# A bigger ring for raw weights, one transpose a step later, and weight loads in front of stores

## The chip, the core and the metric

The kernel runs on one core of a Trainium2 chip. The metric is the device time of one execution in microseconds (us). Five engines work side by side, each through its own list of instructions in order: TensorE (PE, with its weight loads as PEld), VectorE (DVE), ScalarE (ACT), GpSimd (POOL) and SyncE (SP), which here issues nearly all DMA transfers. They wait for each other by semaphores.

## The reference

Attention with a forget-gate bias, then a gated feed-forward layer, then a plain one, on 2304 tokens of width 512:

```python
def _attn_ref(q, k, v, s):                       # q, k, v: (4, 8, 576, 64)
    scores = scale * np.matmul(q, k.transpose(0, 1, 3, 2))
    cum = np.cumsum(np.maximum(s, 0.0), axis=-1)
    bias = -(cum[:, :, :, None] - cum[:, :, None, :])
    scores = np.where(causal, -1000000000.0, scores + np.minimum(bias, 0.0))
    ...                                          # softmax over the last axis
    return np.matmul(attn, v)
def _moe_ref(x, w_gate, w_val, w_out):           # 512 -> 1536 -> 512
    g = x @ w_gate
    silu = g * (1.0 / (1.0 + np.exp(-g)))
    return silu * (x @ w_val) @ w_out
def _moe2_ref(x, w_in, w_out):                   # 512 -> 2048 -> 512
    h = x @ w_in
    return (h * (1.0 / (1.0 + np.exp(-h)))) @ w_out
```

## The kernel before, in words

**Three parts.** The first layer (attention and the gated layer) goes batch by batch, four batches of 576 tokens. The attention of a batch is eight *units*, two for each pair of heads: half A (query tiles 0 to 2) and half B (tiles 3 and 4). The attention of batch 0 runs alone at the start. That of each later batch runs inside the gated layer of the batch before. The second layer comes last.

**Chunks.** The gated layer's weights come in nine chunks for each batch, named c = 0 to 35 over the four batches: six gate-and-value chunks of four steps (`gate`, 24 matmuls of 288 columns a step) and three output chunks of eight steps (`down`, 12 matmuls a step). Each chunk has 96 such matmuls. Every product is made of three matmuls in a 32-bit format, of a high part and a low part of each operand.

**Weights.** They arrive as raw 64-bit words. In the first batch each chunk is loaded as four raw pieces of 512 KB (`w_load`, line 388, or `w_piece`, line 403; tile name `r`, tag `wraw`), decoded one chunk ahead (`decode`: ScalarE at lines 409 and 410, VectorE at lines 412 and 415), cut into high and low parts (`w_cut`: ScalarE at line 112, POOL at line 501, tile `wt`) and stored (`w_store`, line 489). The later batches load them back finished (`w_half`, line 396). From chunk 9 on the second layer's weights are prepared in the same manner in *sets* (`ahead_load`, `ahead`, `u_sum`, `u_cut`), and `u_store` (line 486) writes a set out in four stores.

**Rings.** A pool with n buffers hands out its tiles in turn, and a tile's first writer waits until the last reader of the tile n places earlier is done. Raw pieces, decoded tiles, sums and cut tiles all come from the one ring `raw`. The 32-bit scratch `dk` of the decode comes from the PSUM ring `ps_m` (four banks, shared with the gate and output groups `pgv` and `po`) for chunks 1 to 8, and from the pool `dec` for chunk 0 and for the sets. A gate step takes two banks of `ps_m`. ScalarE's tanh (line 531) and VectorE (lines 532 and 533) empty them. Scores (`psc`, line 218) and transposes (`ptr`, lines 302 to 316) each take the two buffers of the PSUM ring `ps_a`. ScalarE (line 112) and VectorE (line 114) copy the transposes out as `pt`.

**What sets the order.** In the loop over the chunks of the first three batches TensorE's order is that of the code: `at[k]` lists what is put in front of quarter k of chunk c. For the k-th chunk of a batch that is the scores of unit k in front of quarter 0, the values of unit k-2 and the transposes of unit k-1 in front of quarter 2. The order of the other engines is made by a scheduler, which a change in a ring moves too. In the last batch all orders are those of the code: after each step the list `todo` of that step is issued, and then the stores of sets that are ready (`stores`).

Of the kernel before, what the change touches and what calls it, by code (L numbers as in the profile page):

```python
# [66 lines left out]
def kernel(  # L67
# [11 lines left out]
    first_layer = ctx.enter_context(ExitStack())  # L79
    attention = ctx.enter_context(ExitStack())  # L80
    second_layer = ctx.enter_context(ExitStack())

    def pool(name, bufs, space=None, scope=ctx, side="left"):
        kw = {"space": space} if space is not None else {}
        return scope.enter_context(tc.tile_pool(name=name, bufs=bufs, side=side, reuse_waits="tile", **kw))
# [2 lines left out]
    const = pool("const", 1)  # L88
    dram = pool("dram", 1, bass.MemoryType.DRAM)
    wt_p = pool("wt", 4)  # L90
    raw_p = pool("raw", 5, scope=first_layer)
    dec_p = pool("dec", 2, scope=first_layer)
    tmp_p = pool("tmp", 3, scope=first_layer)
    h_p = pool("h", 6, scope=first_layer)
    xt_p = pool("xt", 8, scope=first_layer)
# [1 line left out]
    qkr_p = pool("qkr", 3, scope=attention, side="right")  # L97
    cum_p = pool("cum", 3, scope=attention, side="right")
    e_p = pool("e", 6, scope=attention, side="right")
    z_p = pool("z", 4, scope=attention, side="right")  # L100
    pt_p = pool("pt", 3, scope=attention, side="right")
    zero_p = pool("zero", 1, scope=attention, side="right")
    v_p = pool("v", 2, scope=attention, side="right")
    sm_p = pool("sm", 10, scope=attention, side="right")
    ps_m = pool("ps_m", 4, PS)
    ps_a = pool("ps_a", 2, PS, scope=attention, side="right")

# [181 lines left out]
    def turn_mm(b, g, half):  # L289
        tiles, base, n = HALF[half]  # L290
        es = st.pop((b, g, half, "e"))
        ps = [ps_a.tile([P, 2, 512], F32, tag="a", name="ptr") for _ in range(2)]
        put = []
        for j, tile, o in PLACE[half]:
            k0 = TILES[j][0]
            for i in tiles:
                q0, r = TILES[i]
                if q0 < k0:
                    continue
                for hd in range(2):  # L300
                    x = o + q0 - max(k0, base)
                    nc.tensor.transpose(ps[tile][:, hd, x : x + r], es[i][:r, hd, k0 : k0 + P], ident[:r, :r])  # L302
            off = max(k0, base) - base
            put.append((j, tile, o, off, n - off))
        for i, tile, hd, o in PLACE0[half]:
            q0, r = TILES[i]
            if b == 0:
                for k in range(2):
                    nc.tensor.matmul(
                        out=ps[tile][k * D : k * D + D, hd, o : o + r], lhsT=es[i][:r, k, :D], rhs=ident[:r, :r],  # L310
                        start=True, stop=True,
                    )
                continue
            z = st.pop((b, g, half, "z", i))
            r = P
            nc.tensor.transpose(ps[tile][:, hd, o : o + r], z[:r], ident[:r, :r])
        st[b, g, half, "p"] = (ps, put, [None, None])

    def turned(b, g, half, k):
        n = HALF[half][2]  # L320
        ps, _, pt = st[b, g, half, "p"]
        pt[k] = pt_p.tile([P, 2, 512], F32, tag="pt", name="pt")
        w = WIDE[half][k]
        if w is None:
            copy("av"[k], pt[k][:, 0, :n], ps[k][:, 0, :n])
        else:
            copy("av"[k], pt[k][:, :, :w], ps[k][:, :, :w])
# [156 lines left out]
    def u_store(q, k, e):  # L484
        name, n, *parts = wst["o", q, k]
        return nc.sync.dma_start(out=wu_d[q // 2, "ZSCE".index(name), :, e, :n], in_=parts[e])
# [86 lines left out]
    def chunk_steps(c):  # L573
        kind, i = stream[c]
        if c == 0:
            return [lambda f=f, n=n: gate(c, f, f, *n) for f, n in ((1, both[0]), (0, both[1]), (1, both[1]))]
        if kind == "gv":
            return [lambda f=f, n=n: gate(c, 2 * i + f, f, *n) for f, n in order(2, both, "01"[i == NGV - 1])]
        return [lambda m=m, n=n: down(c, i, m, *n) for m, n in order(KD, both, "1")]
# [162 lines left out]
    def scores(u):  # L742
        x = units[u]
        fetch(u)
        if (*x, "e") not in st:
            masks(*x)
        score_mm(*x)
        for i in HALF[x[2]][0]:
            for f in (score_min, expo, inverse, first_keys, normal):
                f(*x, i)  # L750

    def transpose(u):
        turn_mm(*units[u])
        turned(*units[u], 0)
        turned(*units[u], 1)

    def value(u):
        value_mm(*units[u])
        x_high(*units[u])
        x_low(*units[u])  # L760
# [57 lines left out]
    def body():  # L818
# [48 lines left out]
        for q in range(12):  # L867
            x = 17 * q // 3
# [11 lines left out]
        for c in range(last):  # L880
            b = batch[c]
            cur = chunk_steps(c)
            at = {k: [] for k in range(5)}
            if b + 1 < B:
                k, u0 = c % len(L1), (b + 1) * H
                if k < H:
                    at[1 if c == 0 else 0].append(lambda x=u0 + k: scores(x))
                    if k > 1:
                        at[2].append(lambda x=u0 + k - 2: value(x))
                    if k > 0:  # L890
                        at[2].append(lambda x=u0 + k - 1: transpose(x))
                else:
                    at[1] += [lambda x=u0 + k - 2: value(x), lambda x=u0 + k - 1: transpose(x)]
                    at[3].append(lambda x=u0 + k - 1: value(x))
            for n, stp in enumerate(cur):
                if n == 0:
                    w_ahead(c)
                if n * 4 % len(cur) == 0:
                    todo = events.get(c * 4 + n * 4 // len(cur), [])
                    with tc.issue_after(w_last[0]) if todo else nullcontext():  # L900
                        with tc.issue_after(act_last[0]) if todo else nullcontext():
                            for f in todo:
                                f()
                if c == 0:
                    for p in at[n - 1] if n else []:
                        p()
                elif n * 4 % len(cur) == 0:
                    for p in at[n * 4 // len(cur)]:
                        p()
                stp()  # L910
            for p in at[4]:
                p()
# [6 lines left out]
        stores = []  # L919
        g = nc.gpsimd  # L920
        for c in range(last, n1):
            cur = chunk_steps(c)
            k = c - last
            more = [[] for _ in range(4)]
            extra = []
            if c + 1 < n1:
                more[0] += [lambda e=e: w_half(c + 1, e) for e in range(2)]
            i = tail_pieces.get(c)
            if i is not None:
                more[1].append(lambda i=i: ahead(i))  # L930
                if i % 2:
                    more[1].append(lambda q=i // 2: u_sum(q))
                    for e in range(2):
                        more[2 + e].append(lambda q=i // 2, k=e: u_cut(q, k))
                        more[2 + e].append(
                            lambda q=i // 2, k=e: stores.extend(lambda e=e: u_store(q, k, e) for e in range(2))
                        )
            if c + 1 in tail_pieces:
                more[1].append(lambda i=tail_pieces[c + 1]: ahead_load(i))
            if k == 0:  # L940
                more[2].append(lambda: x2_load(0))
            sub = {1: 1, 2: 2, 4: 3, 5: 4}.get(k)
            cuts = {1: [0], 2: [1], 3: [2, 3], 4: [4], 5: [5], 6: [6]}.get(k, [])
            if sub:
                more[0].append(lambda: x2_sub(0, sub))
            for e, x in enumerate(cuts):
                src = None if x in (0, 2, 5) else {1: 1, 3: 2, 4: 3, 6: 4}[x]
                f = lambda x=x, src=src: x2_cut(0, x, None if src is None else p2["t", src], g)
                if len(cur) == 4:
                    more[2].append(f)  # L950
                else:
                    extra.append(f)
            if k == 7:
                more[3].append(lambda: u_load(1, "Z"))
            if k == 8:
                more[0].append(lambda: u_load(0, "ZS"))
            for n, stp in enumerate(cur):
                if n == 0:
                    wst.pop(c - 1, None)
                stp()  # L960
                todo = more[n] if len(cur) == 4 else more[n // 2] if n % 2 == 0 else extra[n // 4 : n // 4 + n // 2 % 2]
                late, stores[:] = list(stores), []
                for f in todo:
                    f()
                for f in late:
                    f()
# [100 lines left out]
```

## Time and profile before

| | us |
|---|---|
| median of 3 runs | 1007.95 |
| lowest, highest run | 1001.23, 1009.87 |
| profiled execution | 1002.95 |
| its span, first to last instruction | 1001.1 |
| TensorE busy in the span | 989.5 (99%) |
| ScalarE, VectorE, POOL busy | 523.0, 557.0, 592.7 |

The profile is of one execution. Times in it count from the start of the span. A row's busy time is that of its instructions laid over one another. "Idle before" is the time in which the engine had nothing running just before them, and the name behind the arrow is what ended it. In the trace DMA issue rows belong to SP's queue (SPq), and what a transfer takes to land is given apart from them.

### The profile page before, as it was taken

The page shows a single profiled execution, that of the slowest core. Times are in us where ns is not written, and L with a number is a line of the kernel's source. Part 1 is how long each engine was busy: PE and PEld are TensorE (multiplying, and loading weights), DVE is VectorE, ACT ScalarE, POOL GpSimd, SP SyncE. Part 2 cuts the span into 40 slices and gives each one's busy share as a digit, 9 for nine tenths or more (in the row PEclk, how much of TensorE's full clock was granted, in tenths as well). Part 3 has the DMA queues.
Part 4 walks back from the last instruction along what each step waited for, and adds up shares of the span by engine and source line. Part 5 has one row for each costly group of instructions (what it writes and reads, how often), then busy time and mean ns, then how long its engine had stood idle before and what let it go on. Part 6 is the DMA issues. An engine that isn't in the chain of part 4 may idle for free.

```text
span 1001.1 us, 19462 instructions
## 1 busy us (share of the span) xinstructions
PE 989.5 (99%) x6924; PEld 929.8 (93%) x6924; DVE 557.0 (56%) x1408; ACT 523.0 (52%) x1267; POOL 592.7 (59%) x748
## 2 busy tenths in 40 slices
PE   8999999999999999999999999999999999999998
PEld 6588889999998899899899999999999999999998
DVE  6868576635546545535542323366666667665555
ACT  6779888535666436655533443234544335543333
POOL 6967747515867556757542665356567458674445
PEclk9999999999999999999999999999999999999999
DMA  8798879667779799775858776797767866896662
GB/s 240 198 319 301 275 277 301 222 221 246 279 267 294 266 306 311 265 248 214 288 205 330 270 297 258 261 388 278 294 242 281 312 222 249 297 343 232 244 219 113
DMA packets 81616, 267.16 MB, mean 267 GB/s; under 512 B 9904, under 2 KB 29360, under 8 KB 66160
## 3 DMA queue, kind: packets, MB, share of 16 engines
q1 hardware_dynamic: 81328, 265.66, 75.8%
q8 instruction: 54, 0.88, 0.3%
q14 instruction: 42, 0.34, 0.1%
q10 hardware_dynamic: 192, 0.27, 0.1%
HBM read 208.15 MB, written 57.75 MB: 266 GB/s over the span
## 4 chain that ended last, share of the span: by engine, by line
PE 90%; ACT 3%; DMA 3%; DVE 2%; issue 1%; POOL 1%; SPq 0%; DVEq 0%; ACTq 0%; POOLq 0%
PE pgv L522 9%; PE pgv L524 9%; PE pgv L523 9%; PE pu L663 6%; PE pu L666 6%; PE pu L667 6%; PE po L708 6%; PE po L709 6%; PE po L710 6%; PE po L522 5%; PE po L523 5%; PE po L524 5%; PE pv L351 5%; PE psc L218 4%; PE ptr L302 3%; ACT e L255 1%
## 5 line engine op out<-in xcount | busy, mean ns | idle before, releaser
L522 PE MATMUL pgv<-xt,wt 128*128 128x288 f32 x768 | 229.5, 299 | 0.2 <-DVE wraw L415 0.2
L524 PE MATMUL pgv<-xt,wt 128*128 128x288 f32 x768 | 226.1, 294 | 0.0
L523 PE MATMUL pgv<-xt,wt 128*128 128x288 f32 x768 | 226.0, 294 | 0.0
L640 POOL TENSOR_TENSOR h<-u,h 128x384 fp32r<-128x384 f32 x72 | 74.8, 1039 | 142.1 <-ACT h L112 134.5
L522 PEld LDWEIGHTS pgv<-xt,wt 128*128 128x128 f32 x768 | 144.1, 188 | 11.5 <-DVE m L235 6.3
L523 PEld LDWEIGHTS pgv<-xt,wt 128*128 128x128 f32 x768 | 144.1, 188 | 0.0
L524 PEld LDWEIGHTS pgv<-xt,wt 128*128 128x128 f32 x768 | 144.0, 188 | 0.0
L112 ACT ACTIVATE h<-u 128x288 fp32r<-128x288 f32 (+1 forms) x168 | 79.8, 475 | 100.5 <-DVE u L533 99.2
L535 POOL TENSOR_TENSOR h<-u,h 128x288 fp32r<-128x288 f32 x96 | 79.0, 825 | 86.4 <-ACT h L112 84.2
L522 PE MATMUL po<-h,wt 128*128 128x288 f32 x384 | 114.7, 299 | 0.0
L523 PE MATMUL po<-h,wt 128*128 128x288 f32 x384 | 113.1, 294 | 0.0
L524 PE MATMUL po<-h,wt 128*128 128x288 f32 x384 | 113.0, 294 | 0.0
L708 PE MATMUL po<-h,wt 128*128 128x384 f32 x336 | 112.4, 335 | 0.0
L709 PE MATMUL po<-h,wt 128*128 128x384 f32 x336 | 112.3, 334 | 0.0
L710 PE MATMUL po<-h,wt 128*128 128x384 f32 x336 | 112.3, 334 | 0.0
L663 PE MATMUL pu<-x,wt 128*128 128x384 f32 x330 | 111.8, 339 | 0.1
L666 PE MATMUL pu<-x,wt 128*128 128x384 f32 x330 | 111.8, 339 | 0.0
L667 PE MATMUL pu<-x,wt 128*128 128x384 f32 x330 | 111.7, 339 | 0.0
L640 POOL TENSOR_TENSOR h<-t,h 128x384 fp32r<-128x384 f32 x96 | 107.0, 1136 | 5.5 <-ACT h L112 5.5
L669 ACT ACTIVATE s<-pu 128x384 f32<-128x384 f32 x48 | 23.6, 492 | 150.0 <-PE pu L667 150.0
L255 ACT ACTIVATE e<-e,m 64x64 f32<-64x64 f32 (+4 forms) x160 | 88.3, 554 | 25.7 <-DVE m L235 25.0
L719 DVE TENSOR_TENSOR acc<-po,acc 128x384 f32<-128x384 f32 x144 | 76.8, 558 | 36.3 <-PE po L710 35.6
(115 smaller groups left out, 2187.0 us busy)
## 6 DMA issues: line engine op xcount, KB each, us to landing
wt<-w_d SPq DMA_DIRECT2D x54, 1024.0 KB, 6.9
wt<-wu_d SPq DMA_DIRECT2D x48, 1024.0 KB, 9.2
wt<-wu_d SPq DMA_DIRECT2D x47, 768.0 KB, 6.8
r<-in_w_dram SPq DMA_DIRECT2D x36, 512.0 KB, 6.8
w_d<-wt SPq DMA_DIRECT2D x18, 1024.0 KB, 8.5
r<-in_w_dram SPq DMA_DIRECT2D x64, 256.0 KB, 7.1
qkr<-in_qk_dram SPq DMA_DIRECT2D x32, 288.0 KB, 9.0
cumb<-cum_d SPq DMA_DIRECT2D x15, 576.0 KB, 9.2
```

The costliest lines, as they stand in the source:

```text
L112: act_last[:] = [nc.scalar.activation(out=out, in_=in_, func=AF.Copy, scale=scale).ins]
L255: nc.scalar.activation(out=e[:r, hd, :wd], in_=e[:r, hd, :wd], func=AF.Exp, bias=m[hd][:r], scale=-1.0, accum_out=put[hd],)
L522: nc.tensor.matmul(out=ps[:, :n], lhsT=a, rhs=xh, start=(k == 0), stop=False)
L523: nc.tensor.matmul(out=ps[:, :n], lhsT=a, rhs=xl, start=False, stop=False)
L524: nc.tensor.matmul(out=ps[:, :n], lhsT=c, rhs=xh, start=False, stop=(k == last))
L640: nc.gpsimd.tensor_tensor(out=h[:, 1], in0=u, in1=h[:, 0].bitcast(F32), op=ALU.subtract)
L663: nc.tensor.matmul(out=o, lhsT=a, rhs=x[:, 0, kk], start=fresh and kk == 0, stop=False, skip_group_check=True)
L666: nc.tensor.matmul(out=o, lhsT=a, rhs=x[:, 1, kk], stop=False, **more)
L667: nc.tensor.matmul(out=o, lhsT=c, rhs=x[:, 0, kk], stop=kk == 1, **more)
L708: nc.tensor.matmul(out=ps, lhsT=a, rhs=h[:, 0], start=fresh, stop=False, skip_group_check=True)
L709: nc.tensor.matmul(out=ps, lhsT=a, rhs=h[:, 1], stop=False, **more)
L710: nc.tensor.matmul(out=ps, lhsT=c, rhs=h[:, 0], stop=e == 1, **more)
```

## The change

Four edits, all in rings and orders.

The ring `raw` gets six tiles instead of five. The space comes from `dec` (one instead of two), `z` (three instead of four: the scaled first keys of a unit) and `sm` (eight instead of ten small tiles for each of its tags, among them the row maxima `m`).

In chunk 1 the transposes of the second batch's first unit go in front of quarter 3, one gate step later.

In the last batch the stores of a set that become ready in the second half of an output chunk are kept until the first step of the next chunk, where they come behind that step's weight loads.

```diff
-    raw_p = pool("raw", 5, scope=first_layer)
-    dec_p = pool("dec", 2, scope=first_layer)
+    raw_p = pool("raw", 6, scope=first_layer)
+    dec_p = pool("dec", 1, scope=first_layer)
...
-    z_p = pool("z", 4, scope=attention, side="right")
+    z_p = pool("z", 3, scope=attention, side="right")
...
-    sm_p = pool("sm", 10, scope=attention, side="right")
+    sm_p = pool("sm", 8, scope=attention, side="right")
...
                     if k > 0:
-                        at[2].append(lambda x=u0 + k - 1: transpose(x))
+                        at[3 if c == 1 else 2].append(lambda x=u0 + k - 1: transpose(x))
...
-                late, stores[:] = list(stores), []
+                late = []
+                if n < 4:
+                    late, stores[:] = list(stores), []
                 for f in todo:
                     f()
                 for f in late:
                     f()
```

On TensorE, in chunk 1, the transposes `ptr` of the first unit and the gate step around them (rows that repeat are left out):

```order
+L522 MATMUL pgv<-xt,wt 128x288
+L523 MATMUL pgv<-xt,wt 128x288
+L524 MATMUL pgv<-xt,wt 128x288
...
 L302 MATMUL ptr<-ident,e 128x128 x6
 L316 MATMUL ptr<-ident,z_151 128x128
 L316 MATMUL ptr<-ident,z 128x128 x2
-L522 MATMUL pgv<-xt,wt 128x288
-L523 MATMUL pgv<-xt,wt 128x288
-L524 MATMUL pgv<-xt,wt 128x288
```

The 24 matmuls of the third gate step now stand in front of the transposes, not behind them.

On ScalarE, at the end of chunk 0 and the start of chunk 1, where the four raw pieces of chunk 2 (`r_1101`, `r_1103`, `r_1105`, `r_1107`) are decoded. Before:

```order
L409 ACTIVATE wraw<-r_1101 128x512
L409 ACTIVATE wraw<-r_1103 128x512
L112 ACTIVATE h<-u 128x288
L410 ACTIVATE dk<-r_1101 128x512
L410 ACTIVATE dk<-r_1103 128x512
L255 ACTIVATE e,l<-e,m 64x64 x2
...
L409 ACTIVATE wraw<-r_1105 128x512
L410 ACTIVATE dk<-r_1105 128x512
L409 ACTIVATE wraw<-r_1107 128x512
L410 ACTIVATE dk<-r_1107 128x512
```

And now:

```order
L531 ACTIVATE u<-pgv 128x288
L409 ACTIVATE wraw<-r_1105 128x512
L409 ACTIVATE wraw<-r_1107 128x512
L112 ACTIVATE h<-u 128x288
L410 ACTIVATE dk<-r_1101 128x512
L410 ACTIVATE dk<-r_1103 128x512
L255 ACTIVATE e,l<-e,m 64x64 x2
...
L410 ACTIVATE dk<-r_1105 128x512
L267 ACTIVATE l<-l 128x2
L410 ACTIVATE dk<-r_1107 128x512
```

The first pass over the third and fourth piece moved from behind the unit's exponentials (line 255) to the place ahead of line 410 of the first two pieces.

On SP's queue, in the last batch, the four stores of one set and the two weight loads for the next chunk:

```order
+L396 DMA wt<-w_d 128x2048 x2
 L486 DMA wu_d<-cut 128x768
 L486 DMA wu_d<-z_8012 128x768
 L486 DMA wu_d<-cut 128x1024
 L486 DMA wu_d<-s_8141 128x1024
-L396 DMA wt<-w_d 128x2048 x2
```

The loads went from behind the four stores to the front of them. Elsewhere in the last batch no load and store changed places.

## Rows read from the trace of the kernel before

**Rows 1.** The page: span, and busy us (share of span) by engine

```profile
span 1001.1 us, 19462 instructions
PE 989.5 (99%) x6924; PEld 929.8 (93%) x6924; DVE 557.0 (56%) x1408; ACT 523.0 (52%) x1267; POOL 592.7 (59%) x748
```

**Rows 2.** Windows: us, busy (count) by engine, clock, DMA, GB/s; last two: weight-tile rows alone

```profile
75.00:100.00 25.00, 24.06 (x177) 21.63 (x176) 20.73 (x70) 23.56 (x71) 17.93 (x26) 1.00 0.87 301
...
530.00:567.00 37.00, 37.00 (x282) 37.00 (x281) 0.00 (x0) 0.00 (x0) 0.00 (x0) 1.00 0.76 272
86.60:93.00 6.40, 6.40 (x48) 6.31 (x48) 0.00 (x0) 0.00 (x0) 1.61 (x1) 1.00 1.00 377
```

**Rows 3.** TensorE's waits, whole span: waiting line, releaser, total us, times, longest

```profile
PE ptr L302 <- POOL e L116: 3.5, 6, 1.4
...
PE pv L351 <- DVE u L532: 0.6, 1, 0.6
...
PE pgv L522 <- DVE wraw L415: 0.2, 1, 0.2
```

**Rows 4.** TensorE's timeline: start, us, instruction, [idle before, and releaser]

```profile
77.99 0.40 PE L522 MATMUL pgv<-xt,wt 128*128 128x288 f32 x1
...
81.29 0.29 PE L522 MATMUL pgv<-xt,wt 128*128 128x288 f32 x1
...
85.46 1.00 PE L302 MATMUL ptr<-ident,e 128*128 128x128 f32 x4 [0.63 <-POOL e L116]
...
93.07 1.36 PE L218 MATMUL psc<-qkr 64*128 64x64 f32 x12
94.62 0.40 PE L522 MATMUL pgv<-xt,wt 128*128 128x288 f32 x1 [0.19 <-DVE wraw L415]
...
412.22 0.76 PE L351 MATMUL pv<-pt,vz 128*64 128x320 f32 x4 [0.61 <-DVE u L532]
```

**Rows 5.** POOL's timeline in chunk 1

```profile
84.90 0.96 POOL L116 TENSOR_SCALAR e<-e,rl 128x256 f32<-128x256 f32 x2
85.79 2.42 POOL L501 TENSOR_TENSOR wt<-wraw,wt 128x1024 fp32r<-128x1024 f32 x1
```

**Rows 6.** ScalarE's timeline in chunks 0 and 1, and near 404 us

```profile
72.66 0.67 ACT L409 ACTIVATE wraw<-r 128x512 f32<-128x512 f32 x1 [0.98 <-DMA r<-in_w_dram]
...
73.57 1.17 ACT L410 ACTIVATE dk<-r 128x512 uint32<-128x512 uint32 x2
...
77.79 0.65 ACT L409 ACTIVATE wraw<-r 128x512 f32<-128x512 f32 x1
...
87.60 0.81 ACT L112 ACTIVATE pt<-ptr 128x768 f32<-128x768 f32 x1
...
403.77 0.68 ACT L409 ACTIVATE z<-r 128x512 f32<-128x512 f32 x1 [0.83 <-DMA wu_d<-z]
```

**Rows 7.** SP's queue: start and duration of issues, chunk 0 and last batch

```profile
66.09 1.39 SPq L388 DMA_DIRECT2D r<-in_w_dram  x2
67.87 0.92 SPq L489 DMA_DIRECT2D w_d<-wt  x1
68.84 0.42 SPq L388 DMA_DIRECT2D r<-in_w_dram  x1
...
584.46 0.32 SPq L486 DMA_DIRECT2D wu_d<-s  x1
584.90 1.21 SPq L396 DMA_DIRECT2D wt<-w_d  x2
```

**Rows 8.** DMA issues: count, KB each, median us to landing; second row 563 to 600 us

```profile
r<-in_w_dram SPq DMA_DIRECT2D x36, 512.0 KB, 6.8
...
wt<-w_d SPq DMA_DIRECT2D x6, 1024.0 KB, 7.9
```

**Rows 9.** VectorE's timeline in chunks 0 and 1

```profile
76.24 1.28 DVE L415 SCALAR_TENSOR_TENSOR wraw<-r,dk 128x512 uint32<-128x512 uint32 x2
...
80.00 0.68 DVE L415 SCALAR_TENSOR_TENSOR wraw<-r,dk 128x512 uint32<-128x512 uint32 x1
```

## The prediction

> **What bounds the kernel now.** I read the page's first part, then the windows, then TensorE's waits, and last the timelines of the engines that feed it. [Rows 1] say that matmuls are in flight in 989.5 of 1001.1 us, so 11.6 us of the span have none. A busy matmul row is not PE at its peak, so the second thing to see is the pace: in a stretch in which nothing but weight matmuls runs, 282 of them touch 37.00 us, 131 ns each, and in the stretch of the second chunk that the change touches 48 touch 6.40 us, 133 ns each, both at a granted clock of 1.00, the 2.4 GHz level [rows 2]. The matmuls there are already as dense as anywhere; what can be won is idle time, not pace.
>
> [Rows 3] are TensorE's waits over the whole execution, and most of what stands there is out of reach: of the 3.5 us for a scaled probability tile, in six stalls, only one of 0.63 us lies behind the first batch's attention. From the second chunk on I find three stalls in the timelines [rows 4]: 0.63 us at 85.46 in the transposes of the second batch's first unit, 0.19 us at 94.62 where a gate group waits for a PSUM bank that a weight decode still holds, and 0.61 us at 412.22 before a value matmul. Together 1.43 us.
>
> **The change part by part.** No matmul, activation, vector operation or byte of traffic is added or taken away. The change moves instructions and loosens or tightens rings.
>
> *The transpose a step later.* The stall at 85.46 ends when POOL's scaling of a 128x256 piece ends; that piece starts at 84.90 [rows 5], behind other work of POOL. The new place is one gate step of 24 matmuls later, 24 x 133 ns = 3.2 us, which is more than 0.63 us, and POOL's order now has the piece ahead of both weight subtractions, 2.4 us each [rows 5]. So this stall goes: minus 0.63 us. What is late next: the score matmuls of the next unit take the two banks that the transposes filled, so they wait for ScalarE's copy of them. Before, that copy started at 87.60 and the score matmuls at 93.07 [rows 4, 6], 5.5 us of room. Now a single gate step stands between transposes and scores, 3.2 us, and ScalarE's order has ten operations between the last exponential and the copy, where it had none. At 0.81 us for the copy [rows 6] I put the new wait between nothing and 0.9 us.
>
> *The six-tile ring.* Raw words, decoded words and the later split tiles share one ring. With six tiles each raw piece follows the same piece of the chunk before; with five it followed the next one, and a chunk's fourth piece followed a decoded tile that POOL had to finish. [Rows 7] show that: the second and third piece of chunk 2 are issued from 66.09 on, then a store at 67.87 that waits for POOL, and only then the fourth at 68.84. After the change the fourth no longer stands behind that store, so pieces land about a place earlier. At 403.77 a decode waited 0.83 us for a store of the same ring [rows 6], and the late tanh behind it is what holds the value matmul at 412.22; the sixth tile should free it: minus 0.61 us. The bank at 94.62 should be free as well: minus 0.19 us.
>
> The same ring changes ScalarE's order, and here something is paid. In chunk 1 the first decode pass (line 409) of pieces three and four of chunk 2 now stands ahead of line 410 of pieces one and two. Before, it ran at 77.79, long after the data was there. Now it waits for landings: the piece in the issue slot of 66.09 was seen by ScalarE at 72.66 after 0.98 us of waiting [rows 6, 7], the next, issued a microsecond later, lands by the median of 6.8 us [rows 8] at about 73.9. So line 409 of the fourth piece ends near 74.5, and line 410, which started at 73.57 [rows 6], starts near 74.9, 1.3 us late. Who waits for that: VectorE's closing pair, which ran from 76.24 to 77.5 and released its first bank near 76.9, while TensorE wanted it at 77.99 [rows 4, 9], a lead of 1.1 us. A shift of 1.3 us leaves a stall of about 0.2 us. The next bank was released at 80.68 and wanted at 81.29 [rows 4, 9], a lead of 0.6 us, with a second line 412 now ahead of it: about 1.0 us. After that the eviction of step 0 stands behind two more VectorE score operations: up to 0.8 us. With the copy above these make 3.0 us if none overlaps another and nothing if the pieces land a microsecond sooner than I put them. Between these ends I take 1.5 us, because the lead in the rows is of the size of the shift. In the later chunks the same order meets pieces that had a chunk's time to land, and I cost it at nothing; if that cover fails it is the second rival.
>
> ScalarE is where the weight of this lies: in the window of these chunks it is busy 23.56 of 25.00 us [rows 2]. The Trainium skill's page "PSUM — Partial Sum Buffer" (Engine vs sequencer instructions) says that the ScalarE queue is strictly first in, first out, which speaks against an early decode that waits for data; by that rule nothing behind line 409 slips past it, which the 0.98 us wait agrees with, and the sum would be nearer its upper end, plus 1.6 us, than the zero that the leads in the rows give.
>
> *Smaller rings (dec 1, z 3, sm 8).* The single decode tile serves only chunk 0 and the later sets, where one piece's VectorE half is done before the next piece's first half. Four z tiles become three: the last one of a unit now follows the transposes of the unit before, a chunk ahead of its own use. Eight small tiles: one maximum of a unit waits for one exponential. I cost the three at nothing; the cover is one chunk of about 13 us, and if it goes POOL and VectorE have 7 us and 4 us of idle in the window [rows 2].
>
> *The weight loads in front of the set stores.* One place: the pair of loads at 584.90 stood behind stores, the last of which waited for POOL [rows 7]. In front of them the loads can start about 3 us sooner, and land 7.9 us later by the median of that stretch [rows 8]. No TensorE wait in [rows 3] names a transfer, so nothing is gained: 0. The stores then start some 3 us later and hold their ring tiles that long, with one tile more in the ring: 0.
>
> **Sum.** Minus 1.43, plus 1.5 (0 to 3.0): about zero, from minus 1.4 to plus 1.6 us. Against the profiled execution, 1002.95 us with a span of 1001.1 us, that is 1003.0 us. This execution lies 5.0 us below the median of the three runs, 1007.95 us (1001.23 to 1009.87). The middle of all four executions is 1005.45 us, and I forecast the changed kernel there: **1005.5 us**.
>
> **Rivals.**
> - *Only the gains come* (chance 0.28): the pieces land early enough, and the copy finds its gap. For it: the store that held the fourth piece is out of the way. Against it: the 0.98 us wait in a spot that moves forward. Time: 1005.5 - 1.4 = 1004.1 us.
> - *The early decode blocks ScalarE in every chunk* (0.08): line 409 waits for landings in each of the eight decoded chunks, and the evictions queued behind it keep TensorE's banks. It decides from the point where the wait is longer than the 1.1 us lead. At 1.5 us each, 8 x 1.5 = 12 us: 1017.5 us. Against it: the later chunks had no TensorE stall with a later load order.
> - *The busy row hides stalls* (0.04): weight loads are busy 929.8 us, so 71 us have none [rows 1]. If a sixth of that were waiting that the ring ends, 12 us would go: 993.5 us. The Trainium skill's page "Perfetto Trace Analysis" (Identifying the Most-Contended Engine) says that matmul busy time is a poor measure and the weight-load share the better one, which gives this case its room. The pace of 133 against 131 ns speaks against it: hidden waits would be in the pace.
> - My forecast, a trade of small stalls, has 0.60.
>
> **Numbers.** About 1%, 10 us, is what a measurement of this kernel can tell from no change, since its runs already lie 0.9% apart. The forecast and the first rival lie within that: same 0.88; the second rival gives slower 0.08, the third faster 0.04. The range goes from the lowest run less all gains, 1001.23 - 1.43 = 999.8, to the highest run plus the whole cost, 1009.87 + 3.0 = 1012.9; rivals two and three, 0.12, are left out.
>
> **What would show it.** Right: the transposes without a wait on POOL one gate step later; no wait before the value matmul near 412; no TensorE wait for a load near 594; in the second chunk new waits of 0.2 to 1 us for a decoded tile or for an eviction, and perhaps one of the score matmuls for ScalarE's copy. ScalarE waits for raw pieces near 73. Wrong: a TensorE idle sum that differs from 11.6 us by more than 3 us, waits for decodes in many chunks, or a granted clock below 1.00 after a stall.

## The result: slower by 8 us, with ScalarE standing in line for raw weights

| us | before | changed |
|---|---|---|
| median (runs) | 1004.82 (13) | 1012.78 (13) |
| lowest, highest | 1001.23, 1009.87 | 1010.25, 1015.61 |
| profiled execution, span | 1002.95, 1001.1 | 1015.01, 1013.3 |

The ratio is 1.0084 with a 95% interval of 1.0071 to 1.0096: 8.4 us (7.1 to 9.6) slower, where a trade of stalls near zero was forecast. 1012.78 us lies just inside the predicted range, 0.12 us below its end, but only because that range was drawn around the scatter of the first three runs; the direction was missed.

The page of the changed kernel, its span and busy line, answers to [rows 1]:

```profile
span 1013.3 us, 19473 instructions
PE 991.3 (98%) x6924; PEld 931.2 (92%) x6924; DVE 559.8 (55%) x1408; ACT 524.4 (52%) x1267; POOL 592.9 (59%) x748
```

The span grew by 12.2 us. Of these, 10.4 us are time without a matmul (22.0 us in place of 11.6), and 1.8 us are matmuls that took longer. The instruction counts of the five engines in this line are those of [rows 1]. Where the idle time lies is read from windows, which give the length of a stretch and then each engine's busy time. First the stretches of before:

```profile
60.00:185.00 125.00, 124.06 (x955) 111.51 (x954) 87.33 (x253) 101.16 (x251) 76.95 (x109) 1.00 0.83 278
185.00:525.00 340.00, 339.39 (x2642) 310.38 (x2642) 170.27 (x543) 183.09 (x487) 200.80 (x306) 1.00 0.77 262
```

Then the same of the changed kernel:

```profile
60.00:185.00 125.00, 115.12 (x867) 103.51 (x869) 79.48 (x236) 95.44 (x241) 74.30 (x104) 0.99 0.82 269
185.00:525.00 340.00, 340.00 (x2642) 310.56 (x2639) 175.05 (x553) 188.35 (x497) 198.72 (x309) 1.00 0.77 257
```

TensorE idles 9.88 of the 125 us in which the weights are decoded, before 0.94. From 185 to 525 us it has no idle time left, where it had 0.61 us. So the decoded chunks of the first batch lose 8.9 us and the stretch behind them gains 0.6 us. The rest, about 2 us, is 1.2 us in the first 60 us, where the idle time lies between 5.9 and 9.0 us over the executions profiled here (5.9 us with the four pool sizes alone), and 1.0 us behind 525 us. TensorE's waits in the decoded chunks, in the changed kernel (line, releaser, total us, times, longest), answer to [rows 3]:

```profile
PE po L522 <- DVE wraw L415: 2.3, 2, 1.7
PE pgv L522 <- DVE wraw L415: 1.8, 2, 1.0
PE po L522 <- DVE xt L366: 1.7, 1, 1.7
PE pgv L522 <- DVE u L532: 1.6, 2, 1.5
PE pgv L522 <- DVE xt L366: 0.9, 1, 0.9
...
```

The releasers are of several kinds (decoded words, attention values, gate products), and no transfer is among them. Such a list has its cause one engine further back. All of this VectorE work follows a ScalarE operation, so ScalarE's waits in the same stretch come next. Before, the row that matters stands well down the list:

```profile
ACT wraw L409 <- POOL wt L501: 2.1, 3, 1.0
...
ACT wraw L409 <- DMA r<-in_w_dram: 1.5, 2, 1.0
```

In the changed kernel it is at the top:

```profile
ACT wraw L409 <- DMA r<-in_w_dram: 17.1, 10, 4.4
```

Seventeen microseconds of ScalarE are now spent in front of the first decode pass, waiting for a raw piece to land. Nine of the ten waits are on a third or fourth piece; the tenth, 0.57 us at 182.93, is on a second one. The two longest, 4.41 and 4.39 us, are both on a fourth piece; here is the first in ScalarE's timeline of the changed kernel, behind a short wait on the third piece of the same chunk:

```profile
125.50 0.69 ACT L409 ACTIVATE wraw<-r 128x512 f32<-128x512 f32 x1 [0.65 <-DMA r<-in_w_dram]
...
126.47 0.41 ACT L562 ACTIVATE acc<-po 128x288 f32<-128x288 f32 x1
131.29 0.66 ACT L409 ACTIVATE wraw<-r 128x512 f32<-128x512 f32 x1 [4.41 <-DMA r<-in_w_dram]
131.85 0.37 ACT L112 ACTIVATE xt<-pv 128x256 fp32r<-128x256 f32 x1
132.11 0.80 ACT L112 ACTIVATE pt<-ptr 128x768 f32<-128x768 f32 x1
132.81 0.41 ACT L562 ACTIVATE acc<-po 128x288 f32<-128x288 f32 x1
```

Behind line 409 stand three evictions of PSUM, of attention values, of transposes and of an output group. None of them needs the raw piece. The first two had their data for all of the 4.41 us, which begin at 126.88: TensorE had left the values and transposes behind it by 126.06, as its rows below show. VectorE's low half of the values (line 366) follows the first eviction, and TensorE follows VectorE. One row of VectorE:

```profile
132.25 0.42 DVE L366 TENSOR_TENSOR xt<-pv,xt 128x256 fp32r<-128x256 f32 x1 [5.47 <-ACT xt L112]
```

And TensorE: five of its seven stalls in chunks 2 to 8 (the one at the very first step of chunk 2 is read further down), with the first and the last, and the first matmul behind those transposes (126.06):

```profile
115.97 0.40 PE L522 MATMUL po<-h,wt 128*128 128x288 f32 x1 [0.64 <-DVE wraw L415]
...
126.06 0.38 PE L522 MATMUL po<-h,wt 128*128 128x288 f32 x1
132.73 0.40 PE L522 MATMUL po<-h,wt 128*128 128x288 f32 x1 [1.69 <-DVE xt L366]
136.86 0.38 PE L522 MATMUL pgv<-xt,wt 128*128 128x288 f32 x1 [1.00 <-DVE wraw L415]
...
171.59 0.40 PE L522 MATMUL pgv<-xt,wt 128*128 128x288 f32 x1 [0.93 <-DVE xt L366]
176.38 0.60 PE L522 MATMUL po<-h,wt 128*128 128x288 f32 x1 [1.65 <-DVE wraw L415]
```

The seven stalls sum to 7.06 us. The two at 132.73 and 136.86 follow the wait of 4.41 us and sum to 2.69 us, so part of it was covered.

Before, ScalarE met the same work in another order:

```profile
121.62 0.39 ACT L112 ACTIVATE xt<-pv 128x256 fp32r<-128x256 f32 x1 [0.70 <-PE pv L351]
122.39 0.81 ACT L112 ACTIVATE pt<-ptr 128x768 f32<-128x768 f32 x1 [0.38 <-PE ptr L302]
...
126.91 0.67 ACT L409 ACTIVATE wraw<-r 128x512 f32<-128x512 f32 x1
127.49 0.62 ACT L410 ACTIVATE dk<-r 128x512 uint32<-128x512 uint32 x1
128.24 0.67 ACT L409 ACTIVATE wraw<-r 128x512 f32<-128x512 f32 x1
```

There the evictions stand ahead of line 409 of pieces three and four, and ScalarE stands before these two for no longer than 0.13 us (from 128.11, the end of line 410, to 128.24).

How late do the pieces come? SyncE's queue of the changed kernel, the four loads of that chunk:

```profile
114.42 4.05 SPq L388 DMA_DIRECT2D r<-in_w_dram  x3
118.52 0.60 SPq L166 DMA_DIRECT2D qkr<-in_qk_dram  x1
119.52 0.33 SPq L489 DMA_DIRECT2D w_d<-wt  x1
119.96 0.36 SPq L388 DMA_DIRECT2D r<-in_w_dram  x1
```

The fourth piece is issued at 119.96, directly behind a store of 1 MB, and ScalarE sees it at 131.29: 11.3 us, against the median of 6.8 us of the raw loads [rows 8]. ScalarE reached it at 126.88, 6.9 us after the issue. The landing itself is not what the change made worse. Before, the same piece took longer; its issue, and then the time to landing, first of before and then of the changed kernel:

```profile
115.98 0.52 SPq L388 DMA_DIRECT2D r<-in_w_dram  x1
DMA to landing us min/median/max: 12.2/12.2/12.2
DMA to landing us min/median/max: 11.3/11.3/11.3
```

It landed at 128.2, and line 409 of before, at 128.24, came just behind it. What moved is the reader.

### The profile page after: what moved, and what is told of

Read it like the earlier page. It is cut to its first block, busy times and chain, and to the rows that moved or that the text cites. A ratio compares the mean times of both kernels' runs of the same rounds, so it can differ in the third digit from the quotient of the medians.

```text
span 1013.3 us, 19473 instructions
## 1 busy us (share of the span) xinstructions
PE 991.3 (98%) x6924; PEld 931.2 (92%) x6924; DVE 559.8 (55%) x1408; ACT 524.4 (52%) x1267; POOL 592.9 (59%) x748
## 4 chain that ended last, share of the span: by engine, by line
PE 85%; DMA 6%; ACT 4%; DVE 3%; issue 1%; POOL 1%; SPq 0%; DVEq 0%; ACTq 0%; POOLq 0%
PE pgv L522 8%; PE pgv L524 8%; PE pgv L523 8%; PE pu L663 6%; PE pu L667 6%; PE pu L666 6%; PE po L708 6%; PE po L709 6%; PE po L710 6%; PE po L522 5%; PE po L523 5%; PE po L524 5%; PE pv L351 4%; DMA r<-in_w_dram 4%; PE psc L218 3%; PE ptr L302 3%
## 5 line engine op out<-in xcount | busy, mean ns | idle before, releaser
L116 POOL TENSOR_SCALAR e<-e,rl 128x128 f32<-128x128 f32 (+8 forms) x135 | 73.4, 557 | 44.9 <-DVE rl L268 41.4
```

## Experiments

The theory: with six tiles the scheduler's order puts line 409 of pieces three and four ahead of evictions, and ScalarE, which works in order, stands there until the piece lands. The rivals: the later transposes cost it, the order of stores and loads does, or one of the smaller rings does.

**The four pool sizes alone.** The kernel before, with this:

```diff
-    raw_p = pool("raw", 5, scope=first_layer)
-    dec_p = pool("dec", 2, scope=first_layer)
+    raw_p = pool("raw", 6, scope=first_layer)
+    dec_p = pool("dec", 1, scope=first_layer)
-    z_p = pool("z", 4, scope=attention, side="right")
+    z_p = pool("z", 3, scope=attention, side="right")
-    sm_p = pool("sm", 10, scope=attention, side="right")
+    sm_p = pool("sm", 8, scope=attention, side="right")
```

> The kernel before with the four pool sizes of the change alone (raw 6, dec 1, z 3, sm 8); transposes and stores as before. Theory A (the six-tile ring lets the first decode pass of a chunk's third and fourth raw piece stand ahead of ScalarE's other work, and ScalarE then waits for their landing): nearly the whole loss, 6 to 10 us above the kernel before, and ScalarE's waits of line 409 for raw pieces near 17 us in the first 185 us (1.5 us before). Theory B (the transposes a step later leave the next scores too little room): within 2 us of the kernel before. Theory C (the store order in the last batch): within 2 us of the kernel before.

Measured: 1013.48 us, ratio to before 1.0092 (1.0077 to 1.0107). The whole loss is there without the other two edits, and so are ScalarE's waits:

```profile
ACT wraw L409 <- DMA r<-in_w_dram: 16.9, 10, 4.1
```

**The three smaller rings alone**, the raw ring at five:

```diff
-    dec_p = pool("dec", 2, scope=first_layer)
+    dec_p = pool("dec", 1, scope=first_layer)
-    z_p = pool("z", 4, scope=attention, side="right")
+    z_p = pool("z", 3, scope=attention, side="right")
-    sm_p = pool("sm", 10, scope=attention, side="right")
+    sm_p = pool("sm", 8, scope=attention, side="right")
```

> The kernel before with the three smaller pools alone (dec 1, z 3, sm 8), raw still 5. Theory A: within 2 us of the kernel before, since the first decode pass stays behind the exponentials. Rival D (a wait for a z tile or a row maximum is the cost, not the raw ring): 5 to 10 us slower, with ScalarE or VectorE waits on z or m tiles.

Measured: 1005.12 us, ratio 1.0011 (0.9999 to 1.0024), with 2.1 us of ScalarE waits for raw pieces. That is 1.1 us (-0.1 to 2.4), which can't be told from nothing. With the run above, the sixth raw tile, on top of the smaller rings, is what brings the loss. A sixth tile beside the old sizes of the other rings was not run.

**The later transposes and the store order alone**, all pools as before:

```diff
-                        at[2].append(lambda x=u0 + k - 1: transpose(x))
+                        at[3 if c == 1 else 2].append(lambda x=u0 + k - 1: transpose(x))
...
-                late, stores[:] = list(stores), []
+                late = []
+                if n < 4:
+                    late, stores[:] = list(stores), []
```

> The kernel before with the later transposes and the stores behind the loads, all pools as before. Theory A: within 2 us of the kernel before; the stall of 0.63 us at the transposes of the second batch's first unit is gone, and the score matmuls after them wait at most 0.9 us for the copy. Theories B and C: 5 to 10 us slower.

Measured: 1004.27 us, ratio 0.9996 (0.9983 to 1.0008): neither a loss nor a gain that can be seen. The trace shows a trade. The stall of 0.63 us at the transposes is gone and the scores behind them do not wait, but the wait for a decoded tile at the first step of chunk 2, 0.19 us before, has grown:

```profile
95.36 0.40 PE L522 MATMUL pgv<-xt,wt 128*128 128x288 f32 x1 [0.93 <-DVE wraw L415]
```

**The order undone, the ring kept.** The changed kernel, where in chunks 2 to 8 line 409 of pieces three and four is held on ScalarE behind line 410 of the piece before:

```diff
-    act_last = []
+    act_last, dec_last = [], []
...
-            nc.scalar.activation(out=k, in_=lo, func=AF.Copy, scale=0.937 * 2.0**-29)
+            dec_last[:] = [nc.scalar.activation(out=k, in_=lo, func=AF.Copy, scale=0.937 * 2.0**-29).ins]
...
-        wst["k", c, e] = (zz, t, k)
-        unpack(zz, t, k, part)
+        wst["k", c, e], pin = (zz, t, k), 1 < c < len(L1) and e in (2, 3)
+        with tc.issue_after(dec_last[0]) if pin else nullcontext(): unpack(zz, t, k, part)
```

> The changed kernel, all four edits, with one thing more: in chunks 2 to 8 the decode of the third and of the fourth raw piece is queued on ScalarE behind the second pass (line 410) of the piece before it, as it stood in the kernel before. Theory A: the loss goes, within 2 us of the kernel before; ScalarE's waits for raw pieces under 4 us, TensorE's idle time back to about 11 to 13 us. If the ring itself or its loads cost the time (another traffic on the DMA engines, later stores), it stays 5 us or more above the kernel before.

Measured: 1002.77 us, ratio to before 0.9987 (0.9978 to 0.9997). Not only is the loss gone, this kernel is 1.3 us (0.3 to 2.2) faster than before, the lowest median here. The decoded stretch in its windows:

```profile
60.00:185.00 125.00, 125.00 (x966) 112.99 (x965) 89.16 (x260) 101.78 (x253) 78.29 (x109) 1.00 0.82 280
```

TensorE is never idle in it, and the 0.94 us of before are gone too. The instruction counts are those of the changed kernel, and so are the ring sizes; fourteen first passes, two in each of seven chunks, are held back. So neither the ring nor its loads cost the time by themselves.

**Half the dose: only the fourth piece held.** As above, with `e == 3` for `e in (2, 3)`.

> The changed kernel, with the first decode pass of the fourth piece alone held behind the second pass of the third, in chunks 2 to 8; the third piece's stays as early as the scheduler puts it. The waits of over 4 us are all on the fourth piece, the third's are 0.4 to 2.5 us each. If waits for landings are the loss, most but not all of it goes: 1004 to 1008 us, with 3 to 7 us of ScalarE waits for raw pieces left. If both pieces must be held for the order to be good, the time stays above 1010 us; if the third piece costs nothing, it equals the kernel with both pinned, 1003 us.

Measured: 1003.55 us, ratio 1.0000 (0.9989 to 1.0012), 0.45 us below the range expected, between the cases named there. ScalarE still waits 4.2 us for raw pieces, five times and up to 2.1 us, and TensorE idles 0.70 us in the stretch: waits of this size are mostly covered. Whether the third piece costs anything can't be told, since the interval overlaps that of the run with both held.

**The other side: order kept, landing sooner.** The changed kernel, with both stores of a finished chunk behind the four raw loads:

```diff
-    act_last = []
+    act_last, r_last = [], []
...
-                nc.sync.dma_start(out=t, in_=w64[g, :, e * DW : (e + 1) * DW, :])
+                r_last[:] = [nc.sync.dma_start(out=t, in_=w64[g, :, e * DW : (e + 1) * DW, :]).ins]
...
-            w_store(c, e)
...
         if first[c + 2]:
             w_load(c + 2)
+        if first[c + 1]:
+            with tc.issue_after(r_last[0]): [w_store(c + 1, e) for e in range(2)]
```

> The changed kernel, with both stores of a finished weight chunk queued on SyncE behind the four raw loads of the chunk after next, so that no raw piece is queued behind a 1 MB store; ScalarE's order stays of the changed kernel's kind, with the first decode pass of the third and fourth piece early. If the loss is ScalarE standing in order for landings, the fourth piece lands sooner, ScalarE's 17.1 us of waits for raw pieces between 60 and 185 us fall to about 5 to 10 us, and the time lies between before and the changed kernel, 1006 to 1010 us. If the place of the first pass in the order costs by itself, however early the data is, the time stays at 1011 to 1014 us.

Measured: 1008.89 us, ratio to before 1.0048 (1.0033 to 1.0064), in the middle, as forecast. ScalarE's waits fell from 17.1 to 11.4 us, less far than the 5 to 10 us expected. SyncE's queue at the place of the rows above now has the load ahead of the store:

```profile
118.84 0.53 SPq L388 DMA_DIRECT2D r<-in_w_dram  x1
119.42 0.42 SPq L489 DMA_DIRECT2D w_d<-wt  x1
```

And ScalarE's two decode passes there:

```profile
124.42 0.68 ACT L409 ACTIVATE wraw<-r 128x512 f32<-128x512 f32 x1
128.12 0.66 ACT L409 ACTIVATE wraw<-r 128x512 f32<-128x512 f32 x1 [3.01 <-DMA r<-in_w_dram]
```

From issue to ScalarE it is now 9.3 us, 2.0 less than the 11.3 us, and the wait is 3.01 in place of 4.41. No eviction stands between these two passes, where the changed kernel had two (126.47 is the second). So line 409 of the fourth piece comes no later in ScalarE's order than there, and its place alone doesn't make the price: the wait does.

Side by side, with the time in 60 to 185 us that ScalarE waits for raw pieces at line 409 and that TensorE has no matmul (125 us less its busy time there):

| kernel | ScalarE waits, us | TensorE idle, us | ratio to before |
|---|---|---|---|
| both pieces held | 0 (no such wait) | 0.00 | 0.9987 |
| before | 1.5 | 0.94 | 1 |
| fourth piece held | 4.2 | 0.70 | 1.0000 |
| loads ahead of stores | 11.4 | 4.95 | 1.0048 |
| four pool sizes alone | 16.9 | 10.31 | 1.0092 |
| changed | 17.1 | 9.88 | 1.0084 |

The ratios follow the waits (the two last kernels are the same within their intervals). The 4.2 us that are left with the fourth piece held cost nothing that can be told from zero.

## Why the prediction was wrong

**The step that failed** stands in the part on the six-tile ring: "In the later chunks the same order meets pieces that had a chunk's time to land, and I cost it at nothing". They had not. In the rows above the loads of a chunk are issued one after another up to 119.96, the scheduler's order brings ScalarE to line 409 of the fourth piece in the same chunk, 6.9 us after its issue, and the landing took 11.3 us. The cost there was 7.06 us of stalls in place of zero, in the profiled execution. The early decode had been found, and in the one chunk whose order was read it was priced; the same look at the other chunks' order against the same landing times would have shown it.

**The second rival** had the mechanism: the early decode blocks ScalarE in every chunk. It was priced at 12 us, 1.5 us in each of eight chunks, and measured 8.4 us. By its own point of decision not every chunk pays: of the ten waits five are longer than the 1.1 us lead (2.46, 1.14, 1.76, 4.41, 4.39). It got a chance of 0.08 on one argument, that later chunks had no TensorE stall before. That argument was empty, since before the landings were just as late (12.2 us for the fourth piece issued at 115.98), and only the evictions' place ahead of line 409 hid it. The change took just this place away. The sentence on the Trainium skill's page "PSUM — Partial Sum Buffer" (Engine vs sequencer instructions), that ScalarE's queue is strictly first in, first out, agrees with the 4.41 us that evictions stood behind a decode of other data; it should have been applied to eight chunks, not to one.

**Chunk 1** and the first step of chunk 2 came out near the upper end of the 0 to 3.0 us (whose terms, 0.2, 1.0, 0.8 and 0.9, add to 2.9). TensorE's timeline of the changed kernel, against [rows 4]:

```profile
80.27 0.40 PE L522 MATMUL pgv<-xt,wt 128*128 128x288 f32 x1 [1.49 <-DVE u L532]
87.05 0.40 PE L522 MATMUL pgv<-xt,wt 128*128 128x288 f32 x1 [0.16 <-DVE u L532]
90.35 0.82 PE L302 MATMUL ptr<-ident,e 128*128 128x128 f32 x6
...
94.93 1.36 PE L218 MATMUL psc<-qkr 64*128 64x64 f32 x12 [0.28 <-DVE pt L114]
97.08 0.40 PE L522 MATMUL pgv<-xt,wt 128*128 128x288 f32 x1 [0.80 <-DVE wraw L415]
```

Four stalls, 2.73 us, where 1.5 us was taken. The total is nearer than its parts: the first gate step waited 1.49 us for an eviction, where 0.2 us for a decoded tile had been put; the next step, priced at 1.0 us, did not wait; the eviction behind it cost 0.16 us of up to 0.8. The 0.80 us at 97.08 is a wait that was to go. ScalarE waited 2.46 and 0.52 us for the two pieces, not the one microsecond that I had carried over:

```profile
73.34 0.68 ACT L409 ACTIVATE wraw<-r 128x512 f32<-128x512 f32 x1 [2.46 <-DMA r<-in_w_dram]
74.54 0.66 ACT L409 ACTIVATE wraw<-r 128x512 f32<-128x512 f32 x1 [0.52 <-DMA r<-in_w_dram]
```

**The transpose a step later**: right about its own stall. The transposes at 90.35 have no wait in the rows above, and the price foreseen between 0 and 0.9 us for the copy is the 0.28 us at 94.93. It missed another price: with this edit and the store order alone, at five tiles, the wait for a decoded tile at the first step of chunk 2 grew from 0.19 to 0.93 us, by 0.74 us, more than the 0.63 us that went.

**The gains**: two of the three waits are gone, and one of these for a reason that is not shown. The 0.61 us before the value matmul near 412 do not appear (340.00 of 340 us busy), but they are absent as well with a five-tile ring in the run of the transposes and store order, so the sixth tile can't be said to have freed them. The wait for a decoded tile at 94.62 did not go, it grew from 0.19 to 0.80 us. How much of that is the ring and how much the transposes stays open: it is 0.93 us with the transposes and the store order alone and 2.71 us, at 98.12, with the pool sizes alone. With the order held all three go, and that kernel's 1.3 us (0.3 to 2.2) agree with the 1.43 us of the sum.

**"The fourth no longer stands behind that store"**: true for chunk 2, whose four loads now all precede the stores, and wrong as a rule: in four of the seven chunks 2 to 8 (issues at 101.00, 119.96, 158.95 and 180.28) the fourth piece stands behind a store again.

**The smaller rings and the loads ahead of the stores**: costed at nothing, measured at 1.1 us (-0.1 to 2.4) and, with the transposes, at -0.4 us (-1.7 to 0.8). In the last batch the loads did go ahead, as SyncE's queue of the changed kernel shows, and no TensorE wait came or went near them:

```profile
591.03 1.13 SPq L396 DMA_DIRECT2D wt<-w_d  x2
592.26 0.37 SPq L486 DMA_DIRECT2D wu_d<-cut  x1
...
595.91 0.32 SPq L486 DMA_DIRECT2D wu_d<-s  x1
```

In the second layer, at 664.51, there is a wait of 0.65 us that before did not have. Waits of 0.3 to 0.7 us early in that layer stand in all runs with this edit and, 0.3 us, in the one with the smaller rings alone, so whether the edit makes them is open.

**The signs named for "wrong"** came: idle time 10.4 us more where 3 us was the mark, ScalarE's waits for raw pieces in each of seven chunks and TensorE's for decoded tiles at four places, and a granted clock below 1.00 after a stall.

**What can be told from no change** was put at 10 us, from the scatter of single runs. The medians of 13 runs each give an interval of 2.5 us, so that 8.4 us is clear of it.

## What to carry to other kernels

A larger ring can let the scheduler place an in-order consumer earlier, and an operation whose turn comes before its data has landed holds up everything queued behind it. After a change of ring sizes, compare for every chunk the place of the first operation that reads a load with that load's issue time plus its landing time, and count what stands behind it. Where it stands too early, hold the operation behind work that does not need the load, and keep the larger ring: here that turned 8.4 us of loss into 1.3 us of gain (0.3 to 2.2).

## What was not expected of the hardware

A load of 512 KB took 11.3 us to reach its reader when it was issued 0.44 us behind a store of 1 MB, and 9.3 us when issued just ahead of it; the median of these loads was 6.8 us [rows 8]. The other three fourth pieces that the changed kernel issued behind a store landed, by the trace, 7.6, 10.8 and 7.7 us after their issue, and 6.1, 7.9 and 5.7 us in the run with the loads ahead of the stores.

In the decoded chunks of the changed kernel the granted clock fell once, near two short stalls, of 0.93 us at 171.59 and 1.65 us at 176.38. Windows there (the third number from the end is the clock), and then two matmuls:

```profile
174.00:178.00 4.00, 2.35 (x15) 1.84 (x12) 3.97 (x11) 3.16 (x6) 1.06 (x2) 0.80 0.52 154
178.00:182.00 4.00, 4.00 (x25) 4.00 (x25) 3.71 (x18) 3.65 (x14) 3.41 (x3) 0.77 0.83 264
...
177.25 0.44 PE L522 MATMUL po<-h,wt 128*128 128x288 f32 x1
177.49 0.44 PE L523 MATMUL po<-h,wt 128*128 128x288 f32 x1
```

The 0.80 and 0.77 are means of two levels. Read microsecond by microsecond, the clock is 1.00 up to 176, while TensorE stands idle from 174.73 on, 0.50 (the 1.2 GHz level) from 177 to 179, and 1.00 again from 180. At the lower level a matmul follows the one before after 0.24 us. The 15 matmuls from 176.38 to 180.00 took 3.6 us; at 131 ns each [rows 2] they would have taken 2.0, so about 1.6 us, most of the 1.8 us by which the busy time grew. With the four pool sizes alone the loss was as large and the mean clock from 60 to 185 us read 1.00, so the loss does not need the clock.
